# An attention and MLP kernel on one core: a weight load asked for earlier on POOL, and one row's value load moved ahead of a store on SP

## The chip, the core and the metric

The kernel runs on one core of a Trainium2 chip. Its engines are TensorE (PE in the profile; PEld is its weight load), VectorE (DVE), ScalarE (ACT), GpSimd (POOL) and SyncE (SP). Each works through its own instructions in order and waits for the others on semaphores. Transfers are asked for by SP and by POOL, here also once by ScalarE; 16 DMA engines of the core move the bytes. SP's requests and POOL's requests stand in queues of their own (q1 and q0 in the profile). The metric is the time of one execution on the device in microseconds (us); the kernel before takes 300.04 us, the median of 3 runs.

## The reference, cut to what matters

Eight batch rows of 576 tokens go through attention with 8 heads of 64, four of them with a sliding window of 32 and four with a dilated one (every fourth token of 128). The result, 4608 tokens of 512, goes through two matrices with a squared ReLU between them.

```python
mask_plain = (rel >= 0) & (rel < window)
mask_dil = (rel >= 0) & (rel < window * dilation) & (rel % dilation == 0)
masks = np.stack([mask_plain if h < H // 2 else mask_dil for h in range(H)], axis=0)
scores = np.where(masks[None, :, :, :], scores, -1000000000.0)
...
attn = attn / (np.sum(attn, axis=-1, keepdims=True) + 1e-09)
return np.matmul(attn, v).astype(np.float32)
...
h = x @ w_in
r = np.maximum(h, 0.0)
g = r * r
return (g @ w_out).astype(np.float32)
```

q, k and v are float32 of 8 x 8 x 576 x 64, w_in is 512 x 2048 and w_out 2048 x 512, both float32.

## The kernel before

The attention of a batch row is made in parts, and between them stand the matmuls of the MLP, which take chunks of 512 tokens (c = 0 to 8). A chunk first multiplies with w_in (`mm1_tile`, L291), ScalarE takes the ReLU (L300), VectorE squares it (L314, L325), and then it is multiplied with w_out (L332; from chunk 2 on by seven products instead of eight, L443). The order of all work is written out by hand: `run` takes a plan of steps and names ("24:z0" is the first dilated score of a row at step 24), and `pump` puts the matmuls of the MLP between them. No scheduler changes it, so each engine and each queue works in the order of the program text.

A row's q and k come as float16 by POOL's loads, which also convert. For row 0 and row 1 TensorE transposes them (`t_sliding_one`, L573; `t_dilated_one`, L597) into QKTp (sliding) and QKTd (dilated). From row 2 on, `load_whole_sliding_qk` and `keep_dilated_qk` load them, ScalarE and VectorE put the sliding ones in token order (`in_token_order`, tile o, L259 and L261), SP stores that in device memory (`keep_sliding_qk`, dp, L267) and SP's transposing loads bring it back (L279 for QKTd, L275 for QKTp). `turn` issues these steps.

v comes in float32 into two staging tiles, sv for the sliding heads (6 loads for blocks of 96 tokens, `load_sliding_v`, L168) and sd for the dilated ones (`load_dilated_v`: t = 0 at L176, t = 1 at L180, for row 0 also L179). POOL casts them to float16: sv to vp (`cast_own_v` L218, and L222 for the rows that a block shares with the one ahead of it), sd to vd (`cast_dilated_v`, L235, and L237 for the shared rows). There is one sv and one sd, so the loads of the next row wait until POOL has cast the last. The products with v are L693 (sliding, called a0 to a2) and L720 (dilated, d0 and d1 for t = 0, e0 and e1 for t = 1); VectorE divides by the sums (L676, L677), TensorE transposes to x (L742, L757), and ScalarE copies that into xr (L749, L760), which L291 multiplies.

w_in comes in three pieces (`load_w_in`, L192: columns 0 to 511, 512 to 1023, 1024 to 2047) and w_out in four (`load_w_out`, L197), all asked for by POOL and converted to float16. Weights, q, k and POOL's casts so share POOL's program order; v, the stores, the transposing loads and the output share SP's.

`see(x)` (L204) copies one element of x into a tile that nothing reads. It makes POOL wait until x has landed, and so holds back the loads that POOL is asked for behind it. Before this change it is used for row 1's dilated k (L975, ahead of `let_v_go`, which lets SP load row 1's v), and in each chunk for sv and for QKTp ahead of the next row's loads (L1048, L1051).

The order on POOL around the first edit (L896 to L906) is: casts of row 0's first two sliding blocks; two casts of the first half of the dilated v; w_in's first piece; the cast of blocks 2 and 3; w_in's second piece; the shared part; two casts of the second half of the dilated v; w_in's third piece; the casts of blocks 4 and 5. Around the second edit (L990 to L1013), SP's order for row 2 is: dp (two stores), two transposes to QKTd, two to QKTp, sd (two loads), sv (six loads), and then the first output of chunk 0.

Of the kernel before, what the change touches and what calls it, by code (L numbers as in the profile page):

```python
# [17 lines left out]
def kernel(  # L18
# [134 lines left out]
    def load_whole_sliding_qk(b):  # L153
        n = natp.tile([P, HH, 9, D], FP16, name=f"n{b}", tag="n")
        for i, s in ((1, k), (0, q)):
            nc.gpsimd.dma_start(
                out=n[64 * i : 64 * (i + 1)],
                in_=s[b, 0:HH].rearrange("h (p j) d -> p h j d", j=9),
            )
        return n  # L160
# [4 lines left out]
    def load_sliding_v(b, m0=0, m1=NB):  # L165
        for m in range(m0, m1):
            lo = QB * m - PADP
            nc.sync.dma_start(  # L168
                out=sv[PADP:P, m, :, :],
                in_=v[b, 0:HH, lo + PADP : lo + P, :].transpose([1, 0, 2]),  # L170
            )

    def load_dilated_v(b, t):
        vv = v[b, HH:H].rearrange("h (i c) d -> i h (c d)", c=DIL)
        if t == 0:
            nc.sync.dma_start(out=sd[PADD:P, 0, :, :], in_=vv[0:QD])  # L176
            return
        if b == 0:
            nc.sync.dma_start(out=sd[0:PADE, 1, :, :], in_=vv[QD - PADE : QD])  # L179
        nc.sync.dma_start(out=sd[PADE : PADE + QD, 1, :, :], in_=vv[QD:CL])  # L180

    def load_v(b, dilated_first=False):
        if not dilated_first:
            load_sliding_v(b)
        for t in range(2):
            load_dilated_v(b, t)
        if dilated_first:
            load_sliding_v(b)

    def load_w_in(t):  # L190
        f0, f1 = WI[t]
        nc.gpsimd.dma_start(  # L192
            out=wi[t], in_=moe_w_in[:, f0:f1].rearrange("(dh dl) f -> dl dh f", dl=P)
        )
# [7 lines left out]
    def see(landed):  # L202

        nc.gpsimd.tensor_copy(look, landed)  # L204
# [11 lines left out]
    def cast_own_v(b, mp):  # L216
        m = 2 * mp
        nc.gpsimd.tensor_copy(vp[b % 2][:, m : m + 2, :, 0:D], sv[:, m : m + 2, :, :])  # L218

    def cast_shared_v(b, mp):  # L220
        m, m1 = max(2 * mp, 1), 2 * mp + 2
        nc.gpsimd.tensor_copy(vp[b % 2][0:PADP, m:m1, :, 0:D], sv[P - PADP : P, m - 1 : m1 - 1])  # L222

    def cast_sliding_v(b, mp):
        cast_own_v(b, mp)
        cast_shared_v(b, mp)

    def cast_dilated_v(b, t, a):
        c = 2 * a

        def by_class(x):
            return x[:, :, D * c : D * (c + 2)].rearrange("p h (c d) -> p c h d", d=D)

        o = vd[b % 2][:, t, c : c + 2, :, 0:D]
        nc.gpsimd.tensor_copy(o, by_class(sd[:, t]))  # L235
        if t and b > 0:
            nc.gpsimd.tensor_copy(o[0:PADE], by_class(sd[P - PADE : P, 0]))  # L237
# [8 lines left out]
    def keep_dilated_qk(b):  # L246
        d = dpool.tile([2, HH * CL, DIL * D], FP16, name=f"dd{b}", tag="dd")
        for i, src in ((1, k), (0, q)):
            nc.gpsimd.dma_start(
                out=d[i], in_=src[b, HH:H].rearrange("h (i c) d -> (h i) (c d)", c=DIL)  # L250
            )
        return d

    def in_token_order(b, n):
        o = natp.tile([P, 9, HH, D], FP16, name=f"o{b}", tag="o")
        i = n.rearrange("p h j d -> p j h d")
        j = {2: 6, 3: 6, 4: 9}.get(b, 0)
        if j > 0:
            nc.scalar.copy(o[:, 0:j], i[:, 0:j])  # L259
        if j < 9:  # L260
            nc.vector.tensor_copy(o[:, j:9], i[:, j:9])  # L261
        return o

    def keep_sliding_qk(b, o):
        d = dpool.tile([2, S, HH * D], FP16, name=f"dp{b}", tag="dp")
        for i in (1, 0):
            nc.sync.dma_start(  # L267
                out=d[i].rearrange("(p j) x -> p (j x)", j=9),
                in_=o[64 * i : 64 * (i + 1)].rearrange("p j h d -> p (j h d)"),
            )  # L270
        return d

    def transpose_sliding(b, dp):
        for i in (1, 0):
            nc.sync.dma_start_transpose(out=QKTp[b % 2][:, i, :, PADP:], in_=dp[i])  # L275

    def transpose_dilated(b, dd):
        for i in (1, 0):
            nc.sync.dma_start_transpose(out=QKTd[b % 2][:, i, :, KPAD : KPAD + S], in_=dd[i])  # L279
# [321 lines left out]
    def c_dilated_one(b, a, i, p_, eng):  # L601
        copy(
            eng,
            QKTd[b % 2][:, i, a, KPAD : KPAD + S].rearrange("x (c s) -> x c s", s=9),
            p_[:, 0:UW].rearrange("x (s c) -> x c s", c=64),
        )
# [207 lines left out]
    ns0 = [n0[:, 2 * hp : 2 * hp + 2, :] for hp in range(2)]  # L814
# [78 lines left out]
    for a in range(2):  # L893
        t_dilated_one(0, nd0, a, 0, tq[:, a, :])
        c_dilated_one(0, a, 0, tq[:, a, :], nc.scalar)
    cast_sliding_v(0, 0)  # L896
    for a in range(2):
        cast_dilated_v(0, 0, a)
    load_w_in(0)
    cast_own_v(0, 1)  # L900
    load_w_in(1)
    cast_shared_v(0, 1)
# [81 lines left out]
    n, dd = load_whole_sliding_qk(2), keep_dilated_qk(2)  # L984
# [3 lines left out]
            cast_dilated_v(1, t, a)  # L988

    def turn(b, n, dd):  # L990
        dp = keep_sliding_qk(b, in_token_order(b, n))
        if b < 4:
            transpose_dilated(b, dd)
        transpose_sliding(b, dp)
# [13 lines left out]
            parts,  # L1008
        ),
        more=[(25, lambda: turn(2, n, dd))],  # L1010
    )
    load_v(2, True)
    kept[0]()  # L1013


# [23 lines left out]
    for c in range(1, NTOKC):  # L1039
        b = c + 1  # L1040
# [9 lines left out]
        if b + 1 < B:  # L1050
            see(QKTp[b % 2][0:1, 1, 0, PADP : PADP + 1])  # L1051
            if b > CROSS:

                see(xT[(b - 1) % RING][0:1, 1, S - 1 : S])
            n, dd = load_whole_sliding_qk(b + 1), keep_dilated_qk(b + 1)

            def turn_and_load(b=b + 1, n=n, dd=dd):
                turn(b, n, dd)
                load_dilated_v(b, 0)
                load_dilated_v(b, 1)  # L1060
                if b > 3 and b <= CROSS:
                    load_sliding_v(b)

            if b + 1 > 3:
                transpose_dilated(b + 1, dd)
            if b == 3:
                load_sliding_v(3)
            more.append((ORDER[c], turn_and_load))
            if b >= CROSS:
                more.append((38, lambda b=b + 1: load_sliding_v(b)))  # L1070
# [38 lines left out]
```

## Time and profile before

| what | us |
|---|---|
| the runs | 300.04, 299.71, 300.9 |
| the profiled execution | 301.48 |
| its span in the profile | 299.7 |
| first matmul with w_in starts | 20.17 |
| last matmul ends | 296.54 |

The span runs from the first to the last instruction that the profile shows. The busy time of TensorE counts a matmul from its start to an end that is modelled. Mean shares tell little here, as the kernel has a beginning that waits for the first loads, a long dense middle and an end. By page 2, the clock granted to TensorE is full throughout, and the DMA engines are busy for most of the first 200 us:

```profile
PEclk9999999999999999999999999999999999999999
DMA  7999999799999888998999799989124130003013
GB/s 129 205 159 214 210 212 159 154 174 263 196 195 241 179 154 148 215 270 176 186 229 251 144 169 186 255 187 166 72 92 24 39 131 11 0 2 141 3 35 105
```

Each of the 40 slices is 7.5 us. The page's groups of the loads that the change moves, with their number, size and median time from issue to landing:

```profile
sv<-in_v_dram SPq DMA_DIRECT2D x48, 96.0 KB, 4.9
sd<-in_v_dram SPq DMA_DIRECT2D x16, 288.0 KB
...
wi<-in_moe_w_in_dram POOLq DMA_DIRECT2D x2, 512.0 KB, 6.6
wi<-in_moe_w_in_dram POOLq DMA_DIRECT2D x1, 1024.0 KB, 10.2
...
ns<-in_k_dram POOLq DMA_DIRECT2D x2, 144.0 KB, 6.7
```

In a line of a timeline or of the chain, the first number is the start in us from the span's start and the second the length; a bracket at its end gives the idle time of that engine just before, and what ended it.

### The profile page before, as it was taken

The numbers are of one execution on the slowest core, as the hardware profiler recorded it, in microseconds if no ns is written. First come the engines' busy times: TensorE is split into PE (matmuls) and PEld (weight loads), VectorE is DVE, ScalarE is ACT, GpSimd is POOL, SyncE is SP. The second block draws the span as 40 slices with busy tenths as digits, with TensorE's granted clock in tenths as the row PEclk, the third lists the DMA queues.
The fourth block names the chain that finished last, engine by engine and source line by source line (L and its number), as shares of the span: only waits on it lengthen the run. The fifth ranks groups of instructions, "written<-read, shape, count | busy, mean of one in ns | idle before, by whom it ended". The sixth has DMA issues, their size and how long they took to land.

```text
span 299.7 us, 7125 instructions
## 1 busy us (share of the span) xinstructions
PE 287.7 (96%) x2880; PEld 202.7 (68%) x2880; DVE 202.3 (67%) x371; ACT 176.2 (59%) x331; POOL 96.6 (32%) x153
## 2 busy tenths in 40 slices
PE   2899999999999998999999999999999999999995
PEld 2678945565554577656889988558765875785584
DVE  7686646778633997499688867896878624733662
ACT  1668854778548773766646657664766267425611
POOL 8492009403914604752563019308400000000000
PEclk9999999999999999999999999999999999999999
DMA  7999999799999888998999799989124130003013
GB/s 129 205 159 214 210 212 159 154 174 263 196 195 241 179 154 148 215 270 176 186 229 251 144 169 186 255 187 166 72 92 24 39 131 11 0 2 141 3 35 105
DMA packets 73969, 45.59 MB, mean 152 GB/s; under 512 B 56720, under 2 KB 67600, under 8 KB 73744
## 3 DMA queue, kind: packets, MB, share of 16 engines
q1 hardware_dynamic: 66544, 31.37, 49.0%
q0 software_dynamic: 7248, 13.63, 25.7%
q8 instruction: 22, 0.36, 0.5%
q10 hardware_dynamic: 144, 0.13, 0.1%
q14 instruction: 11, 0.09, 0.1%
HBM read 36.83 MB, written 16.52 MB: 178 GB/s over the span
## 4 chain that ended last, share of the span: by engine, by line
PE 72%; DMA 11%; POOL 6%; DVE 5%; issue 2%; SPq 1%; ACT 1%; POOLq 0%; DVEq 0%; ACTq 0%
PE PS L291 34%; PE PS L443 25%; PE PS L332 6%; DMA nd<-in_k_dram 5%; DMA sv<-in_v_dram 3%; DMA sd<-in_v_dram 3%; PE PS L720 2%; PE PS L693 2%; PE PS L653 1%; POOL vp L222 1%; DVE AT L623 1%; POOL vp L218 1%; ACT AT L619 1%; DVE S L429 1%; PE PS L638 1%
## 5 line engine op out<-in xcount | busy, mean ns | idle before, releaser
L291 PE MATMUL PS<-xr,wi 128*128 128x512 f16 (+3 forms) x704 | 133.5, 341 | 0.3 <-ACT xr L749 0.2
L300 ACT ACTIVATE rt<-PS 128x512 f16<-128x512 f32 (+2 forms) x160 | 88.4, 557 | 42.9 <-PE PS L291 40.0
L291 PEld LDWEIGHTS <-wi 128*128 128x128 f16 x704 | 75.8, 113 | 38.5 <-issue 0.5
L325 DVE TENSOR_TENSOR g<-rt 128x1024 f16<-128x1024 f16 (+1 forms) x64 | 45.7, 714 | 28.6 <-ACT rt L300 28.3
L619 ACT ACTIVATE AT<-PS 128x576 f16<-128x576 f32 x64 | 38.4, 652 | 15.5 <-PE PS L653 8.0
L443 PEld LDWEIGHTS <-S 128*128 128x128 f16 x448 | 42.8, 98 | 6.0 <-issue 0.6
L443 PE MATMUL PS<-T,S 128*128 128x256 f16 x336 | 39.6, 273 | 0.0
L443 PEld LDWEIGHTS <-g 128*128 128x128 f16 x336 | 32.2, 98 | 5.6 <-DVE g L325 0.4
L235 POOL CAST vd<-sd 128x512 f16<-128x512 f32 x32 | 23.6, 762 | 36.8 <-DMA sd<-in_v_dram 36.0
L332 PE MATMUL PS<-wo,g 128*128 128x512 f16 x128 | 33.1, 379 | 0.0
L443 PE MATMUL PS<-wo,g 128*128 128x256 f16 x224 | 26.6, 273 | 0.1
L218 POOL CAST vp<-sv 128x512 f16<-128x512 f32 x24 | 17.2, 716 | 23.3 <-DMA sv<-in_v_dram 16.3
L677 DVE TENSOR_TENSOR y<-PS,rcp 72x512 f16<-72x512 f32 (+1 forms) x32 | 22.0, 687 | 1.1
L623 DVE TENSOR_TENSOR AT<-AT,maskd 128x1152 f16<-128x1152 f16 x14 | 11.5, 818 | 15.2 <-ACT AT L619 15.1
L623 DVE TENSOR_TENSOR AT<-AT,maskp 128x1152 f16<-128x1152 f16 x14 | 14.5, 1036 | 10.3 <-ACT AT L619 10.3
L677 DVE TENSOR_TENSOR x<-PS,rcp 96x512 f16<-96x512 f32 (+1 forms) x25 | 16.6, 665 | 0.9
L222 POOL CAST vp<-sv 32x512 f16<-32x512 f32 (+1 forms) x24 | 16.7, 697 | 1.5
L720 PEld LDWEIGHTS <-AT 128*128 128x128 f16 x256 | 11.9, 100 | 6.8 <-DVE y L677 2.0
L332 PEld LDWEIGHTS <-g 128*128 128x128 f16 x128 | 10.3, 98 | 8.0
L429 DVE TENSOR_TENSOR S<-g,S 128x1024 f16<-128x1024 f16 x14 | 10.7, 804 | 7.4 <-PE PS L443 7.4
L676 DVE RECIPROCAL rcp<-PS 96x8 f32<-96x8 f32 (+3 forms) x57 | 11.2, 197 | 4.9 <-PE PS L720 2.9
L443 PE MATMUL PS<-T,g 128*128 128x256 f16 x112 | 14.2, 273 | 0.0
(93 smaller groups left out, 283.2 us busy)
## 6 DMA issues: line engine op xcount, KB each, us to landing
out_dram<-c SPq DMA_DIRECT2D x12, 512.0 KB
sv<-in_v_dram SPq DMA_DIRECT2D x48, 96.0 KB, 4.9
sd<-in_v_dram SPq DMA_DIRECT2D x16, 288.0 KB
dp<-o SPq DMA_DIRECT2D x12, 288.0 KB
wo<-in_moe_w_out_dram POOLq DMA_DIRECT2D x4, 512.0 KB, 14.3
n<-in_k_dram POOLq DMA_DIRECT2D x6, 288.0 KB, 6.0
n<-in_q_dram POOLq DMA_DIRECT2D x6, 288.0 KB, 6.8
dd<-in_k_dram POOLq DMA_DIRECT2D x6, 288.0 KB, 8.1
```

The lines of the kernel that those rows point to most:

```text
L218: nc.gpsimd.tensor_copy(vp[b % 2][:, m : m + 2, :, 0:D], sv[:, m : m + 2, :, :])
L222: nc.gpsimd.tensor_copy(vp[b % 2][0:PADP, m:m1, :, 0:D], sv[P - PADP : P, m - 1 : m1 - 1])
L235: nc.gpsimd.tensor_copy(o, by_class(sd[:, t]))
L291: nc.tensor.matmul(ph[:, o : o + b - a], w_in_of(dmk, ffc), xr[:, dmk, a:b], start=(dmk == 0 and o == 0), stop=(dmk == NDM - 1 and o + b - ...
L300: nc.scalar.activation(rt, ph[:, 0:w], ACTF.Relu)
L325: nc.vector.tensor_mul(g[:, f2 : f2 + 2, o:TOKC], rt[:, :, o:TOKC], rt[:, :, o:TOKC])
L332: nc.tensor.matmul(po, g[:, ffc, o + t * P : o + (t + 1) * P], w_out_of(ffc), start=(ffc == 0), stop=(ffc == NFF - 1),)
L443: nc.tensor.matmul(po[t], lhs(j)[:, t * P : (t + 1) * P], rhs(j), start=j == 0 and not on_top, stop=j == HF - 1, skip_group_check=on_top,)
L619: nc.scalar.activation(AT[:, u + i, 0:UW], ps[:, :, 0 : UW // 2], ACTF.Exp, scale=scale)
L623: nc.vector.tensor_mul(AT[:, u : u + n, 0:UW], AT[:, u : u + n, 0:UW], mask,)
L677: nc.vector.tensor_tensor(out=x, in0=pv[:, :, :, 0:D], in1=rcp[0:w, 0:i, 0:j].unsqueeze(3).to_broadcast([w, i, j, D]), op=ALU.mult,)
L720: nc.tensor.matmul(pav[:, e, h * (D + 2) : h * (D + 2) + D + 1], AT[:, 4 + 2 * a + t, off : off + P], vd[b % 2][:, t, 2 * a + e, h, 0 : D ...
```

## The change

There are two edits. The first puts `load_w_in(0)`, w_in's first piece, ahead of the two casts of the first half of row 0's dilated v on POOL, and ahead of it a `see` of the last sliding k of row 0 (ns0[1], partition 64, where k lies). POOL's order is then: casts of the first two sliding blocks, `see`, w_in's first piece, the two dilated casts, and the rest as before.

The second splits row 2's load of v. The two loads of its dilated half are asked for in `turn`, behind the reordering copies of q and k and ahead of their store; what `load_v(2, True)` asked for behind the transposes is now the sliding half alone. SP's order is then: sd (two loads), dp (two stores), QKTd and QKTp (four transposes), sv (six loads). Other rows keep theirs.

```diff
     cast_sliding_v(0, 0)
+
+    see(ns0[1][64:65, 0, 0:1])
+    load_w_in(0)
     for a in range(2):
         cast_dilated_v(0, 0, a)
-    load_w_in(0)
     cast_own_v(0, 1)
     load_w_in(1)
...
     def turn(b, n, dd):
-        dp = keep_sliding_qk(b, in_token_order(b, n))
+        o = in_token_order(b, n)
+        if b == 2:
+            for t in range(2):
+                load_dilated_v(b, t)
+        dp = keep_sliding_qk(b, o)
         if b < 4:
             transpose_dilated(b, dd)
         transpose_sliding(b, dp)
...
-    load_v(2, True)
+    load_sliding_v(2)
     kept[0]()
```

## The prediction

> **What bounds the kernel now.** I read the page's busy times first, then TensorE's load by stretches, then TensorE's waits, and from each wait the chain back to what releases it.
>
> ```profile
> PE 287.7 (96%) x2880; PEld 202.7 (68%) x2880; DVE 202.3 (67%) x371; ACT 176.2 (59%) x331; POOL 96.6 (32%) x153
> ```
>
> TensorE is busy for 287.7 of 299.7 us, so 12.0 us of idle is all that earlier data could ever give. The same view cut into stretches says where it lies: 6.2 us before the first matmul with w_in (20.17), 0.61 from 20 to 60, nothing from 60 to 108, 1.47 from 108 to 136, 0.45 from 210 to 215, and 3.2 after the last matmul (296.54). The first and last parts wait for the first q and k, for the short chain of row 0, and for the last store; neither edit shortens them. The other idle, 2.53 us, is the ceiling for a gain. Three waits matter, by the timeline (start, length, engine, work, and in brackets the idle before it and what ended it):
>
> ```profile
> 20.17 1.14 PE L291 MATMUL PS<-xr,wi 128*128 128x288 f16 x8 [0.21 <-ACT xr L749]
> 51.88 0.41 PE L693 MATMUL PS<-vp,AT 128*128 128x65 f16 x8 [0.19 <-POOL vp L222]
> 113.29 0.29 PE L693 MATMUL PS<-vp,AT 128*128 128x65 f16 x4 [0.51 <-POOL vp L222]
> ```
>
> The first matmul with w_in is released by ScalarE's copy of x, not by w_in. The other two are released by POOL's casts of v, so what moves v's landing moves them. For row 1 the chain of waits runs back through two long pieces (start, length, what):
>
> ```profile
> 22.14 15.44 DMA nd<-in_k_dram
> ...
> 38.34 6.55 DMA sv<-in_v_dram
> ```
>
> The load of row 1's dilated k stands behind all the weights; when it has landed, `see` (L975) lets POOL free v's loads. Its 15.44 us are queueing: from 16 to 46 us the DMA share is about 1.0 to 1.26 at some 200 GB/s. Ahead of that there is a hole, by the view of 1 us stretches (busy of each engine, then clock, DMA share, GB/s):
>
> ```profile
> 13.00:14.00 1.00, 1.00 (x40) 0.94 (x39) 0.66 (x2) 0.74 (x2) 1.00 (x3) 1.00 0.84 228
> 14.00:15.00 1.00, 1.00 (x14) 0.54 (x14) 1.00 (x3) 0.64 (x1) 1.00 (x2) 1.00 0.63 126
> 15.00:16.00 1.00, 1.00 (x17) 0.71 (x16) 0.96 (x3) 0.60 (x1) 1.00 (x2) 1.00 0.72 24
> 16.00:17.00 1.00, 1.00 (x15) 0.54 (x14) 0.97 (x3) 0.27 (x2) 0.89 (x3) 1.00 0.91 146
> ```
>
> v's loads run dry at about 14.2 and w_in's first bytes come at about 16.1, 2.3 us after their issue at 13.79.
>
> **Part one: w_in's first piece.** POOL before, timeline:
>
> ```profile
> 7.65 0.40 POOL L222 CAST vp<-sv 32x256 f16<-32x256 f32 x1
> 12.44 1.39 POOL L235 CAST vd<-sd 128x512 f16<-128x512 f32 x2 [4.40 <-DMA sd<-in_v_dram]
> 13.79 0.79 POOL L192 DMA_DIRECT2D wi<-in_moe_w_in_dram  x1
> 14.56 0.73 POOL L218 CAST vp<-sv 128x512 f16<-128x512 f32 x1
> ```
>
> Added is one `see`, a copy of one element: 0.18 by the like row at 37.63, 0.24 with the gap behind it. It waits for the last sliding k, issued at 4.54, whose time to landing is 7.3 us (the answer for tile ns: 7.3 and 7.6 for the two issues of that pair; the page's median for k, 6.7, lies between 6.1 and 7.3), so 11.84, 0.48 before sd's 12.32. The piece is then issued at 11.94 + 0.24 = 12.18 instead of 13.79, 1.6 earlier. POOL's 4.40 of idle covers the wait. Behind the waiting `see` stand all of POOL's later casts and loads: the two casts of vd begin at 12.18 + 0.79 = 13.0 instead of 12.44, the first ends at about 13.65, the second at 14.4. Their readers are the products d0 at 13.90 and d1 at 15.29 on TensorE: margins 0.25 and 0.9, so no cost; without that cover each 0.1 that the k lands late costs 0.1. From L218 on POOL is 0.15 earlier (14.4 for 14.56), as it worked in what was idle.
>
> The piece's bytes start at about 12.18 + 2.3 = 14.5, where v's loads end, and fill the hole: all that queues behind moves by up to 1.6. The second piece, issued at 15.1, is ready by 17.4, before the first is through (14.5 + 3.3 = 17.8, from 16.1 to 19.4 before), so the stream doesn't break. Weights gain nothing directly: the pieces landed at 19.39, 22.85 and 28.04, ahead of their first use at about 19.8, 23.5 and 29.5. Row 1's dilated k lands at about 36.0, v's casts end 1.6 earlier, and the wait of 0.19 at 51.88 is gone. Bounds: 0 and -0.19 there; I take -0.19. What the trace does not show is how w_in's bytes and v's last loads share the engines; its lower bound is no cost (the loads are through by then), its upper bound is in the third rival, +2.0. I take 0, as w_in's own row shows 2.3 us from issue to bytes.
>
> **Part two: row 2's dilated v.** Two loads of 288 KB leave SP's queue at 66.14 (0.50 + 0.40, 0.95 with gaps) and go ahead of the store of row 2's q and k.
>
> ```profile
> 56.57 1.19 SPq L267 DMA_DIRECT2D dp<-o  x2
> 57.87 3.92 SPq L279 DMA_TRANSPOSE QKTd<-dd  x2
> 61.89 4.15 SPq L275 DMA_TRANSPOSE QKTp<-dp  x2
> 66.14 0.50 SPq L176 DMA_DIRECT2D sd<-in_v_dram  x1
> 66.69 0.40 SPq L180 DMA_DIRECT2D sd<-in_v_dram  x1
> 67.14 4.05 SPq L168 DMA_DIRECT2D sv<-in_v_dram  x6
> ```
>
> The moved loads wait for POOL's last cast of row 1 (ends 55.66 now, about 54.1 with part one). SP stood waiting for the reordered copy o for 10.6 us before 56.57, so their issue is hidden; were POOL not earlier, the store would slip by 0.05. Their 0.59 MB take 2.8 us at 210 GB/s, from about 56, of which the stretches from 55 to 58 moved 27, 0 and 74 GB/s. The store's bytes may come 1.1 later. Its reader, the transposes at 61.89, wait for TensorE, not for it; their bytes are through by 65 (4 GB/s from 65 to 66), and TensorE first reads QKTp at 72.32, so 6 us cover it.
>
> Sliding v of row 2 starts 1.0 earlier and without 0.59 MB ahead. POOL then doesn't stand 14.70 for sd; its two casts (1.90) go to about 59. The `see` on sv, at 73.38, moves by 1.0 at least and 2.8 at most; I take 2.1. So row 3's load (74.34) comes at about 72.2 and its q at 78 instead of 80.07 (74.97 + 5.1). ScalarE waits for it:
>
> ```profile
> 80.19 1.47 ACT L259 COPY o<-n 128x1536 f16<-128x1536 f16 x1 [2.79 <-DMA n<-in_q_dram]
> 80.20 0.55 DVE L261 COPY o<-n 128x768 f16<-128x768 f16 x1
> 81.68 1.93 SPq L267 DMA_DIRECT2D dp<-o  x2
> ```
>
> ScalarE's half ends at 81.66 and holds the store; VectorE's half is in its busy order and stays at 80.75. So the store gains at most 0.85. From there one link follows the other: transposes, `see` on QKTp (90.89), row 4's loads, whose dilated k is issued at 92.74 and lands 11.8 later, SP's transpose that stood 8.5 us for it (104.59), row 3's sliding v (107.39), its casts (111.83), TensorE at 113.29. The engines are full from 92 to 102, but the same bytes start 0.85 sooner, so I let the link hold. It covers TensorE's idle of 0.12 and 0.51 there. Bounds: 0 if the landing doesn't move, -1.47 if all the idle up to 136 goes; I take -0.63, since the later idle is released by VectorE.
>
> **Sum:** -0.19 + 0 - 0.63 = -0.8. Against the profiled execution's own 301.48 us (span 299.7, 1.78 around it) 300.7. That execution lies 1.44 above the median of 300.04, for which it makes 299.2.
>
> **Rivals.** First, the links break and only the 0.19 is left: 299.85. For it: row 4's loads share the engines with output stores that wait for ScalarE, not for loads. Against it: the engines stood idle at 81 to 83 and at 103 to 106.
>
> Second, more comes: with row 3's v in time the ring of TensorE, ScalarE and VectorE from 113 to 136 loosens and what VectorE releases later goes too: -0.19 - 1.47 - 0.45 = -2.1, so 297.9. For it: these waits stand on one chain behind 113.29. Against it: VectorE is itself busy for 3.97 of 4.00 us from 128 to 132.
>
> Third, slower: w_in takes the engines from v's last loads. Place: the cast of v's blocks 2 and 3 (L218 at 14.56), which landed at 13.3 and 13.6 (5.02 + 8.3, 5.42 + 8.2). Should w_in's bytes start right behind the issue, at 12.97, and go first for all of their 3.3 us, block 3 lands at 16.9; its cast ends at 17.6, the second piece's issue at 18.4, the shared cast (L222, end 16.65 before) at 19.0. TensorE reads that for block 2 at about 17.0, the ninth of its twelve products from 16.68: +2.0 on the way to x and to 20.17, and then on all that follows; 302.0 without the gains, 301.2 with both. It decides from a landing of block 3 later than 14.9 (14.9 + 0.73 + 0.79 + 0.6 = 17.0). Against it: w_in's 2.3 us from issue to bytes.
> The Trainium skill (DMA: Bandwidth & Descriptors, section Queues, rings and completion order) says that each DMA engine takes turns packet by packet between the queue rows that have work. By that rule nothing would go first: block 3's last 0.63 us would take 1.26, its landing be 14.2 and this rival cost nothing, which lowers its chance; whether the bytes of the two meet at all, the trace of before cannot show.
>
> That the change doesn't do what it says has a place too: should sd land ahead of that k, the piece's issue merely delays the casts; this is inside the third rival.
>
> **How the numbers follow.** Forecast 0.44 (own range 298.7 to 299.7), links break 0.15, more 0.22, slower 0.19. The range 297.9 to 301.2 reaches from the second rival to the third with both gains kept. I call 0.5%, 1.5 us, what a measurement can tell from no change; the three runs of before alone spread over 1.2. Faster, below 298.54: most of the second rival (0.19) and the forecast's edge (0.08), 0.27. Slower, above 301.54: the third rival with the gains lost, 0.14. Between: 0.59.
>
> **What would show it.** The piece issued near 12.2 and no hole in the DMA at 15; no wait on TensorE before 20 and its first matmul with w_in at 20.2 (right) or up to 22 (third rival); row 1's dilated k at 36; no wait at 51.9; sd's loads ahead of the store at 54 to 56, QKTp unwaited; row 3's load at 72, the store at 80.8, row 4's dilated k near 103.7 and no wait for vp near 113. A gap on TensorE near 14 (vd late) or at 68 to 72 (QKT late) would make it wrong, and so would a landing of row 4's dilated k that stays at 104.5.

## The result, and the profile after

The changed kernel takes 299.21 us, the median of 22 runs (298.36 to 300.38). The kernel before, run 22 times beside it, takes 300.16 us (299.23 to 301.33). The ratio is 0.9965, with a 95% interval from 0.9951 to 0.9978: a gain of 0.35%, or about 1.05 us. (A ratio here is an estimate from the single runs, not the quotient of the two medians, which is 0.9968.) It is smaller than 0.5%, so by the bound set in the prediction it counts as no change that a few runs could tell, and 299.2 was forecast. The profiled execution of the changed kernel took 299.97 us, with a span of 298.2 (before 301.48 and 299.7). One run in this document, 303.69 us among the 12 of the last kernel of the experiments, was in a slower state, and the ratio there is made without it.

The page's busy times:

```profile
PE 287.3 (96%) x2880; PEld 203.0 (68%) x2880; DVE 202.5 (68%) x371; ACT 176.4 (59%) x331; POOL 98.0 (33%) x154
```

The engines do the same work; POOL has one instruction more, the `see`. Of the 1.5 us between the two spans, 1.1 is idle time of TensorE (12.0 before, 10.9 after); the other 0.4 is in the modelled length of the same 2880 matmuls.

The timeline of POOL after the change (start, length, engine, line, work, and in brackets the idle before it and what ended it):

```profile
11.70 0.22 POOL L204 COPY look<-ns 1x1 f16<-1x1 f16 x1 [3.67 <-DMA ns<-in_k_dram]
11.86 0.79 POOL L192 DMA_DIRECT2D wi<-in_moe_w_in_dram  x1
12.69 1.47 POOL L235 CAST vd<-sd 128x512 f16<-128x512 f32 x2
14.11 0.83 POOL L218 CAST vp<-sv 128x512 f16<-128x512 f32 x1
...
35.58 0.18 POOL L204 COPY look<-nd 1x1 f16<-1x1 f16 x1 [8.40 <-DMA nd<-in_k_dram]
...
69.67 0.18 POOL L204 CAST look<-sv 1x1 f16<-1x1 f32 x1 [10.44 <-DMA sv<-in_v_dram]
70.52 0.64 POOL L156 DMA_DIRECT2D n<-in_k_dram  x1
...
108.22 0.81 POOL L218 CAST vp<-sv 128x512 f16<-128x512 f32 x1 [9.06 <-DMA sv<-in_v_dram]
```

Both edits do what they say. w_in's first piece is issued at 11.86 (13.79 before; 12.18 was forecast). Row 1's dilated k has landed at 35.6 (37.6 before). Row 3's load of k comes at 70.52 (74.34), and the cast of row 3's sliding v at 108.22 (111.83).

The stretches of 1 us after the change (TensorE, its weight load, VectorE, ScalarE, POOL, then the clock, the DMA share and GB/s) show that the hole in the transfers at 14 to 16 is gone:

```profile
14.00:15.00 1.00, 1.00 (x14) 0.50 (x13) 0.97 (x3) 0.17 (x1) 1.00 (x3) 1.00 1.25 231
15.00:16.00 1.00, 1.00 (x15) 0.50 (x12) 0.83 (x3) 0.48 (x1) 0.95 (x2) 1.00 1.25 208
```

Before, these two stretches moved 126 and 24 GB/s.

SP's queue after the change:

```profile
54.04 0.30 SPq L176 DMA_DIRECT2D sd<-in_v_dram  x1
54.44 0.42 SPq L180 DMA_DIRECT2D sd<-in_v_dram  x1
56.22 1.18 SPq L267 DMA_DIRECT2D dp<-o  x2
57.51 3.96 SPq L279 DMA_TRANSPOSE QKTd<-dd  x2
61.56 2.97 SPq L275 DMA_TRANSPOSE QKTp<-dp  x2
64.58 3.47 SPq L168 DMA_DIRECT2D sv<-in_v_dram  x6
...
80.40 1.12 SPq L267 DMA_DIRECT2D dp<-o  x2
...
101.39 2.78 SPq L279 DMA_TRANSPOSE QKTd<-dd  x2
104.27 4.38 SPq L168 DMA_DIRECT2D sv<-in_v_dram  x6
```

The two loads of sd go out while SP would stand waiting for o; the store behind them leaves at 56.22, a little earlier than before (56.57). Row 3's store moves from 81.68 to 80.40, and the transposes that wait for row 4's dilated k from 104.59 to 101.39. What now limits that store is seen in the two halves of o, on ScalarE and on VectorE:

```profile
76.97 1.47 ACT L259 COPY o<-n 128x1536 f16<-128x1536 f16 x1
79.80 0.54 DVE L261 COPY o<-n 128x768 f16<-128x768 f16 x1
```

ScalarE's copy has no wait in brackets any more (2.79 for q before) and ends at 78.44; VectorE's ends at 80.34, and the store leaves 0.06 later.

TensorE's waits in its timeline after the change:

```profile
13.35 0.60 PE L720 MATMUL PS<-vd,AT 128*128 128x65 f16 x8 [0.26 <-POOL vd L235]
19.59 1.14 PE L291 MATMUL PS<-xr,wi 128*128 128x288 f16 x8 [0.30 <-ACT xr L749]
51.30 0.43 PE L693 MATMUL PS<-vp,AT 128*128 128x65 f16 x8 [0.31 <-DVE x L677]
113.97 0.31 PE L653 MATMUL PS<-QKTd 64*128 64x72 f16 x8 [0.44 <-DVE x L677]
```

The two waits for POOL's vp (0.19 at 51.88, 0.51 at 113.29) are gone, and near both places there is one for VectorE's x. A new wait of 0.26 for vd stands at 13.35. From 108 to 136 TensorE is idle for 1.06 us instead of 1.48.

A pair of profiles can't carry a difference of 1 us here. The first transposes of row 0's sliding k on TensorE (L573) start at 8.46 in this execution and at 9.39 in the one of before, though neither edit stands ahead of that k. Which part of the time came from which edit is a question for runs of each edit alone.

### The profile page after: what moved, and what is told of

Its sections match the earlier page's. It is cut to its first block, busy times and chain, and to the rows that moved or that the text cites. A ratio compares the mean times of both kernels' runs of the same rounds, so it can differ in the third digit from the quotient of the medians.

```text
span 298.2 us, 7125 instructions
## 1 busy us (share of the span) xinstructions
PE 287.3 (96%) x2880; PEld 203.0 (68%) x2880; DVE 202.5 (68%) x371; ACT 176.4 (59%) x331; POOL 98.0 (33%) x154
## 4 chain that ended last, share of the span: by engine, by line
PE 81%; DMA 7%; DVE 4%; issue 2%; POOL 2%; SPq 1%; ACT 1%; POOLq 0%
PE PS L291 38%; PE PS L443 24%; PE PS L332 9%; DMA sv<-in_v_dram 5%; PE PS L720 3%; DMA ns<-in_k_dram 2%; PE PS L693 2%; PE PS L638 2%; PE PS L653 1%; POOL vp L218 1%; PE PS L742 1%; DVE AT L623 1%; POOL vp L222 1%; ACT AT L619 1%; SPq L168 1%
## 5 line engine op out<-in xcount | busy, mean ns | idle before, releaser
L332 PEld LDWEIGHTS <-g 128*128 128x128 f16 x128 | 10.3, 97 | 8.0
```

The source lines that it names most:

```text
L332: nc.tensor.matmul(po, g[:, ffc, o + t * P : o + (t + 1) * P], w_out_of(ffc), start=(ffc == 0), stop=(ffc == NFF - 1),)
```

## The experiments

Each result below is a median of 12 runs beside 17 to 35 of the kernel before on the same chip, with the ratio to it and the ratio's 95% interval; the ratio differs from the quotient of the two medians by up to 0.18%. A wait comes from one profiled execution.

**Each edit alone.** The first kernel has only the first edit, the second only the second.

```diff
 e1: turn and load_v(2, True) as before; see and load_w_in(0) ahead of the casts
 e2: casts and load_w_in(0) as before; row 2's dilated v in turn
```

> The first edit alone. Theory (each edit shortens one chain, 0.19 and 0.63 us): 0.2 us faster than before, ratio 0.9985 to 1.000; POOL's casts of row 1's v end 1.5 to 2 us earlier, TensorE's wait of 0.19 for vp near 52 is gone, the waits for vp near 112 to 113 (0.12 and 0.51) are still there, and row 4's dilated k lands where it did (104.5). Rival (the profile of the changed kernel has its first matmul with w_in at 19.59 instead of 20.17, and that comes of the first edit): 0.6 us or more faster, ratio 0.998 or less, first matmul again at 19.6. Rival (the v loads are pushed back): slower, the shared cast of v later than 17.

> The second edit alone. Theory: 0.6 to 0.9 us faster, ratio 0.997 to 0.998; the wait of 0.19 near 52 stays, the wait for vp near 113 is gone or under 0.1, row 3's load at 71 to 72 instead of 74.3, row 4's dilated k lands 1 to 3 us earlier; sd's loads leave SP at 55.7, as POOL's casts of row 1 end where they did. Rival (the gain comes of the first edit): ratio 0.9995 to 1.0005. Rival (the second edit needs the first, since without it sd's loads hold row 2's store): the store slips past 56.6 and less than 0.3 us is gained.

The first edit alone: 300.5 against 300.65, ratio 1.0007 [0.9982, 1.0032]. The second alone: 299.93 against 300.65, ratio 0.997 [0.9947, 0.9993]. TensorE's timeline with the first edit alone:

```profile
13.43 0.59 PE L720 MATMUL PS<-vd,AT 128*128 128x65 f16 x8 [0.53 <-POOL vd L235]
...
111.72 0.29 PE L693 MATMUL PS<-vp,AT 128*128 128x65 f16 x4 [0.26 <-POOL vp L222]
```

The wait at 51 for vp is gone, one of 0.26 near 112 stays, and TensorE loses 0.53 for vd, since POOL now issues w_in ahead of that cast. With the second edit alone:

```profile
50.97 0.41 PE L693 MATMUL PS<-vp,AT 128*128 128x65 f16 x8 [0.27 <-POOL vp L222]
...
111.56 0.29 PE L693 MATMUL PS<-vp,AT 128*128 128x65 f16 x4 [0.26 <-POOL vp L222]
```

Row 3's load is at 71.43 and its store at 80.04, as the theory has it, but 0.26 of the wait for vp at 112 is still there, where under 0.1 had been expected. So the second edit carries the gain that can be measured. The product of the two ratios, 0.9977, lies at the upper edge of the interval of the change (0.9951 to 0.9978).

**Does the second edit's gain pass through row 3's load?** If it does, holding that load back with everything else as changed must undo it. POOL repeats five casts that it has just made, ahead of the loads of row 3's q and k.

```diff
-            for cast in casts[:2]:
+            first = casts[:2]
+            for cast in first:
                 cast()
...
+            if c == 1:
+                for i in range(5):
+                    first[i % 2]()
             n, dd = load_whole_sliding_qk(b + 1), keep_dilated_qk(b + 1)
```

> The changed kernel with row 3's load of q and k held back: POOL repeats five casts that it has just made (the same values to the same places, about 3.3 us) between its looks and that load, which so leaves at 73.8 instead of 70.5, near its time before the change (74.3). Theory (the second edit gains through row 3's load, store, row 4's load and then row 3's sliding v): most of the gain goes, ratio to before 0.998 to 1.000, row 3's store at 81.2 or later, and TensorE's waits for vp near 112 are back. Rival (the gain comes of the traffic that the edit takes out of the stretch from 66 to 70, whatever row 3's load does): ratio 0.9955 to 0.9975.

It took 301.3 against 300.26, ratio 1.0036 [1.0008, 1.0064]: all of the gain is gone and 0.36% more, where 0.998 to 1.000 had been expected. Row 3's load is at 74.46, its store at 82.56, a little later than in the kernel before (74.34 and 81.68). The timeline of ScalarE and TensorE:

```profile
81.06 1.47 ACT L259 COPY o<-n 128x1536 f16<-128x1536 f16 x1 [4.89 <-DMA n<-in_q_dram]
...
78.08 0.41 PE L720 MATMUL PS<-vd,AT 128*128 128x65 f16 x8 [0.29 <-POOL vd L237]
...
112.50 0.29 PE L693 MATMUL PS<-vp,AT 128*128 128x65 f16 x4 [0.51 <-POOL vp L222]
```

TensorE's waits by what it waited for, from 108 to 136 (in all, times, longest), in this kernel:

```profile
PE PS L693 <- POOL vp L222: 0.5, 1, 0.5
PE PS L757 <- DVE y L677: 0.4, 1, 0.4
PE PS L742 <- DVE x L677: 0.3, 1, 0.3
PE PS L720 <- DVE y L677: 0.2, 1, 0.2
```

and in the changed kernel:

```profile
PE PS L653 <- DVE x L677: 0.4, 1, 0.4
PE PS L757 <- DVE y L677: 0.4, 1, 0.4
PE PS L720 <- DVE y L677: 0.2, 1, 0.2
```

The held kernel's list is, row for row, what the same view of the kernel before gives, with sd still ahead of the store and w_in's piece still early. The edit is not clean: the repeated casts also hold back POOL's later casts of row 2's v, and TensorE waits 0.29 for vd at 78.08, which no other profile shows. That is 0.1%, where the ratio moved by 0.7% (0.9965 to 1.0036). So the gain does hang on row 3's load, as far as TensorE's waits account for the casts, and the rival (less traffic from 66 to 70, ratio 0.9955 to 0.9975) is out. That it goes on from there through row 3's sliding v is supported by the list and not isolated: a second profile of the kernel before, shown below, has no wait for vp near 112 at all.

**Is it row 3's sliding v that waits there?** In the kernel before, that load is asked for behind SP's transposes of row 4, which wait for row 4's dilated k. Here the two change places and nothing else does.

```diff
-            if b + 1 > 3:
-                transpose_dilated(b + 1, dd)
             if b == 3:
                 load_sliding_v(3)
+            if b + 1 > 3:
+                transpose_dilated(b + 1, dd)
```

> The kernel before with one other change: SP asks for row 3's sliding v ahead of the transposes that wait for row 4's dilated k (L279 at 104.59), so at about 96 instead of 107.4. It removes the wait for vp near 113 by itself. Theory (that wait and what hangs on it are worth 0.6 us): ratio 0.997 to 0.9985, waits of 0.12 and 0.51 gone. Rival (the wait is only passed on to VectorE's work behind it): ratio 0.9995 to 1.0005. Rival (v's 0.59 MB in front of row 4's dilated k make its transposes late): slower, a wait for QKTd near 115.

It took 300.04 against 300.26, ratio 0.9975 [0.995, 1.0]. The load is asked for at 94.16, the cast of v runs at 104.71 (111.83 before), and the wait near 112 is gone, although row 3's load (73.16) and store (80.91) stay where the second profile of the kernel before has them (73.27 and 80.97). The size, 0.25%, is near what the second edit brings; but the interval reaches 1 and the two medians differ by 0.07% alone, so a gain is not shown.

**Is there more behind it?** If more came from an earlier v or k, further moves of the same kind would add to the gain. One kernel asks for row 3's dilated v early too:

```diff
         o = in_token_order(b, n)
-        if b == 2:
+        if b in (2, 3):
             for t in range(2):
                 load_dilated_v(b, t)
...
                 turn(b, n, dd)
-                load_dilated_v(b, 0)
-                load_dilated_v(b, 1)
+                if b > 3:
+                    load_dilated_v(b, 0)
+                    load_dilated_v(b, 1)
```

> The changed kernel with row 3's dilated v, too, ahead of its store, into the hole in the DMA engines at 78 to 81. Theory (after the change TensorE no longer waits for row 3's v, and VectorE releases what is left of its idle at 112 to 136): no gain over the changed kernel, within 0.2 us, though row 4's dilated k lands 1 to 3 us earlier. Rival (what is left of the idle still hangs on that landing): 0.4 to 1 us faster than the changed kernel.

Row 4's transposes are at 98.67 and row 3's sliding v is cast at 104.94, another 3.3 us earlier, and the ratio is 0.9962 [0.994, 0.9983], like the change itself. A second kernel joins the order of the run before (row 3's sliding v first) to the change, without its `see`:

> The changed kernel without the look ahead of w_in, and with row 3's sliding v asked for ahead of the transposes that wait for row 4's dilated k. Theory (the second edit and this order of SP remove the same wait near 113, so they don't add): ratio 0.995 to 0.9975, as the changed kernel. Rival (they add up): 0.994 or below, the waits of TensorE from 108 to 136 under 0.5 us in sum.

It took 298.99 against 300.5, ratio 0.9959 [0.994, 0.9977]. The two remedies don't add by anything that these runs can tell. With row 3's sliding v cast at 103.25, the waits left from 108 to 136 are all VectorE's (g, x and y), and TensorE is idle there for 1.06 us, as in the changed kernel's profile above. That speaks against the prediction's second rival. The idle itself scatters too much to say more: it is 0.61 in a second profile of the changed kernel and 0.59 with row 3's dilated v early.

**Does w_in's piece take the engines from v?** The prediction's slower rival. Without the `see` the piece is asked for as early as POOL can, in the midst of v's loads.

```diff
-    see(ns0[1][64:65, 0, 0:1])
     load_w_in(0)
```

> The changed kernel without the one-element copy that waits for the last sliding k: w_in's first piece is asked for at about 8.1 instead of 11.9. Theory of the third rival (w_in's bytes take turns with the q, k and v that are still on their way): sd, which landed at 12.3, and the last sliding q land up to 3.3 us later (w_in's own time on the engines), TensorE's first matmul with w_in moves by 0.5 to 3 us, and the kernel is 0.5 to 3 us slower than the changed one. Rival (the engines have room, the copy only costs): as fast as the changed kernel or 0.2 us faster, as the casts of sd then start with its landing.

It took 299.13 against 300.65, ratio 0.9964 [0.9944, 0.9984]: no loss against the changed kernel, where the third rival expected 0.5 to 3 us. POOL's timeline:

```profile
12.48 1.17 POOL L235 CAST vd<-sd 128x512 f16<-128x512 f32 x2 [3.69 <-DMA sd<-in_v_dram]
...
17.05 1.17 POOL L235 CAST vd<-sd 128x512 f16<-128x512 f32 x2 [1.27 <-DMA sd<-in_v_dram]
...
19.43 0.62 POOL L218 CAST vp<-sv 128x512 f16<-128x512 f32 x1 [0.52 <-DMA sv<-in_v_dram]
```

The piece was issued at 8.00, and the bytes do meet: in the profiles of before and of the change the last two of these casts (16.72 and 18.58, 16.36 and 18.21) wait for nothing. But it shows as delays of 1.27 and 0.52 on POOL, and on TensorE as 0.22 for vd at 13.14 and 0.25 for vp at 20.77, not as 3.3 us of v standing behind w_in. The Trainium skill (DMA: Bandwidth & Descriptors, section Queues, rings and completion order) says that an engine takes turns between the queue rows packet by packet; the trace agrees: from 15.0 to 16.5 POOL's queue moved 162 packets (0.17 MB) and SP's 161 (0.05 MB). So v's loads are stretched, and not held back for the whole of a piece; and so is the piece, which landed 10.97 us after its issue, at 18.97, against 17.89 in the changed kernel. What the `see` was to guard against costs nothing that 12 runs can tell.

**What is scatter?** The kernel before was run as if it were a new one, and the changed kernel too.

> The kernel before once more, for its own scatter and a second profile. Theory (the 0.6 us by which the first matmul with w_in starts earlier in the changed kernel's profile is scatter of the first loads' landing, which no edit touches): ratio 0.998 to 1.002, and the first matmul with w_in at 19.2 to 20.2; q and k of row 0 land within 1 us of the first profile's times. Rival (it is the edit's): first matmul at 20.1 to 20.2 again.

> The changed kernel once more, to stand beside the next two on one chip. Theory: ratio to before 0.995 to 0.998, as before; in its profile TensorE waits 0.2 to 0.5 us for vd near 13.3 if row 0's sliding k lands early (transposes of it at 8.3 to 8.6), and not if it lands late (9.3).

The kernel before against itself: 301.0 against 300.26, 1.0016 [0.999, 1.0042]. The changed kernel again: 299.44 against 300.5, 0.9968 [0.9947, 0.9989]. The profiles teach more than the times. TensorE in the second profile of before:

```profile
16.22 0.29 PE L693 MATMUL PS<-vp,AT 128*128 128x65 f16 x4 [0.28 <-POOL vp L222]
...
22.51 1.66 PE L291 MATMUL PS<-xr,wi 128*128 128x288 f16 x12 [0.41 <-DMA wi<-in_moe_w_in_dram]
...
51.07 0.41 PE L693 MATMUL PS<-vp,AT 128*128 128x65 f16 x8 [0.27 <-POOL vp L222]
```

Here the first sliding k is transposed at 8.32 instead of 9.39 and the first matmul with w_in starts at 18.71 instead of 20.17, even earlier than the 19.2 that had been expected. The same kernel now waits for w_in's second piece and, at 16.22, for the shared cast of v, and not at all for vp near 112 (the nearest wait is 0.18 for VectorE's x). From 108 to 136 TensorE is idle for 0.88 us here and 1.48 in the first profile, and for 1.06 and 0.61 in the two profiles of the changed kernel: that stretch scatters by as much as it gains. What is steadier is the time from the first matmul with w_in to the end of the span: 279.5 and 279.4 us in the two profiles of the kernel before, 278.6 and 278.3 in those of the changed kernel, 279.1 with the first edit alone, 278.9 with the second alone and 280.2 with row 3's load held. The second profile of the changed kernel had its k at 8.59 as well, but also an earlier `see` (11.17 for 11.70), so that no wait for vd appeared, against what I had expected of it.

**Is the first edit worth anything?** One kernel keeps w_in where it was and moves the dilated v of rows 2 and 3; one puts the piece between the two casts, for the same two rows; one drops the `see`, for the same two rows.

```diff
 e10: casts, then load_w_in(0), as before; if b in (2, 3)
 e8:  cast_dilated_v(0, 0, 0); load_w_in(0); cast_dilated_v(0, 0, 1); if b in (2, 3)
 e12: load_w_in(0) without see, then the casts; if b in (2, 3)
```

> Dilated v ahead of its store for rows 2 and 3, and w_in's first piece where it was before the change. Theory (the second edit is the whole gain, the first gives back at vd what it gains at vp; row 3's move adds nothing): ratio 0.996 to 0.998, within 0.15% of the changed kernel on the same chip. Rival (the first edit is worth its 0.2 us or more): 0.998 or above. Rival (the first edit costs its wait for vd): 0.9955 or below.

> Both edits, row 3's dilated v ahead of its store too, and w_in's first piece asked for between the two casts of sd, with no look ahead of it. Theory (w_in ahead of both casts makes TensorE wait 0.2 to 0.5 us for vd near 13.3): the first cast starts when sd lands, that wait is gone, and the kernel is 0.1 to 0.4 us faster than the changed one, ratio to before 0.995 to 0.9965. Rival (the wait is taken up by the copies of x that release the first matmul with w_in anyway): as the changed kernel, 0.9965.

> The changed kernel without the look ahead of w_in and with row 3's dilated v ahead of its store, too: the two variants whose profiles were shortest, together. Theory (once row 3's v is in time, VectorE sets the order from 112 to 136, and the start of the kernel differs by the landing of its first loads alone): ratio to before 0.995 to 0.9975, no better than either. Rival (each takes its own 0.2 us): 0.994 or below.

They took 299.57 against 300.5, 299.98 against 300.26 and 299.23 against 300.92; the ratios are 0.9962 [0.9944, 0.998], 0.9973 [0.9948, 0.9997] and 0.9943 [0.9921, 0.9965]. All three intervals overlap, and none lies apart from that of the change. The second ratio is above the range that had been expected, the third below it. The first kernel stands on one chip with the changed kernel's second run: 299.57 and 299.44. TensorE with w_in late:

```profile
23.51 0.68 PE L291 MATMUL PS<-xr,wi 128*128 128x288 f16 x4 [1.23 <-DMA wi<-in_moe_w_in_dram]
```

Of the five profiles with the piece at its old place, two waited on TensorE for w_in (0.41 and 1.23); of the nine with it earlier, none did, but three of these waited for vd (0.22 to 0.53). The median doesn't show whether that nets a gain. The last kernel has the lowest ratio of all; it isn't shown to beat the changed kernel, whose interval reaches from 0.9951.

## Why the prediction held, and where its steps did not

The forecast of -0.8 us came out at about -1.05 (0.35% of 300.16), so the sum is right within its error. That 299.2 was met almost exactly is luck: the kernel before came out at 300.16 and not at the 300.04 that the forecast was taken from. The terms are less right than their sum.

**The second edit, 0 - 0.63: right in its chain, with links sized too small.** Every sign that the prediction listed for it came, some earlier than forecast: sd at 54 to 55, the store unhurt, row 3's load at 70.52 (72.2 was forecast), no wait of ScalarE for q, VectorE's half as the limit of the store, row 4's dilated k at 101.4 (103.7 was forecast), no wait for vp near 113. Holding row 3's load undoes the gain. The term alone measured -0.3% [-0.53, -0.07], some 0.9 us; 0.63 lies inside, so the term isn't shown to be too small, but its links are. The mis-sized one is "So the store gains at most 0.85" and what was built on it: the store moved by 1.28, in the first pair of profiles and in the second (80.97 to 79.69), as VectorE's half didn't stay at 80.75 but ended at 80.34. The v behind it came 3.6 us earlier in the first pair (111.83 to 108.22) and 2.35 in the second (109.78 to 107.43), and not 0.85. Part of the 3.6 is scatter: row 4's dilated k took 11.8 us to land in the first profile of before and 10.4 in the second, with 10.3 and 10.0 in the changed kernel. The wait for vp near 113 was 0.51 in one profile of before and absent in the other. How much of the 0.9 lies outside this one wait isn't settled.

**The first edit, -0.19: its wait went, its gain did not show.** The measured 1.0007 allows from -0.54 to +0.96 us. All five profiles with the old order wait for vp near 51 (0.19 to 0.43), and of the nine with the piece earlier one does (0.19, without the `see`). Two statements failed. "Margins 0.25 and 0.9, so no cost" was read from an execution whose first k came 0.9 us late, when TensorE reached d0 at 13.90. With the k at its more common time TensorE is ready by 12.9 to 13.1, and the wait was 0.26 in the changed kernel and 0.53 with the first edit alone. "Weights gain nothing directly" came from the same execution: with TensorE earlier, w_in's second piece is on the edge, and two profiles with the old order waited 0.41 and 1.23 for it. These two errors have opposite signs. And the 0.19 at 51.88 was no net gain in the end: TensorE stood 0.31 at the same place for VectorE's x, in both profiles of the changed kernel and in three of its variants (0.31 to 0.34). Two readings of the trace were wrong, with no effect on the sum. Row 1's dilated k doesn't stand behind all the weights: two of w_out's four pieces are asked for behind it (23.18 and 28.34). And the 2.3 us "from issue to bytes" are the time until the rate rises: POOL's queue moves its first packets of w_in about 1.5 us after the issue, 18 of them from 15 to 16.

**The rivals.** As ratios to 300.04 they are 0.9994 (the links break, 299.85), 0.9929 (more comes, 297.9) and 1.004 or more (slower), and all three lie outside the measured 0.9951 to 0.9978. That the links break is further refuted by the held load. More did not come with further moves either: with row 3's sliding v cast 6.9 and 8.6 us earlier than before (104.94 and 103.25 against 111.83), no more was gained that can be measured. The last kernel of the experiments (0.9943, from 0.9921) alone leaves room for it. That w_in takes the engines from v's last loads is refuted by the run without the `see`, in which it was given the best chance: the piece went out 4 us earlier than in the change, its packets took turns with v's instead of going first, and TensorE lost 0.2 to 0.25 twice.

**The signs at the start** were half right. The piece came near 12.2 and the hole at 15 closed, as said; the first matmul with w_in came at 19.59 and not at 20.2, and there was a wait before 20. The prediction had named a gap on TensorE near 14 for vd as a sign that it is wrong, and this gap came, 0.26 at 13.35; it was too small to turn the sum. As the kernel before has its first matmul with w_in at 18.71 in its second profile, that start tells when k lands and is no effect of the change.

## What to carry to other kernels

When a queue works in order, look for a load that stands behind an instruction which waits for something else: here moving 0.59 MB ahead of a store that SP was idle for anyway, with no byte less to move, was worth 0.3% (0.07 to 0.53). Follow such a gain through every link to the wait that ends, hold one link back to test it, and expect the next engine to set the rest. A margin below 1 us in the first 20 us of this kernel can't be read from one profile: look at a second execution before an edit is costed at nothing there.

## What the runs showed of the hardware

- The landing of the very first loads varies between executions by about 1 us with nothing changed ahead of it: TensorE's first transposes of the sliding k start between 8.32 and 9.39 over 14 profiles, two of which (9.39 and 9.34) are late; the other twelve lie between 8.32 and 8.85. The late start of the first matmul with w_in follows it (20.17 and 20.38 against 18.69 to 19.59 in the others), and which wait shows up in the first 25 us changes with it.
- w_in's 512 KB asked for in the midst of v's loads slowed those by 1.27 and 0.52 us at the places where POOL waited, and not by the whole length of the piece. While both had work, from 15.0 to 16.5, the two queues moved the same number of packets (162 and 161), and so POOL's, with the larger packets, three times the bytes (0.17 and 0.05 MB).
- A load asked for earlier into busy engines need not land earlier: w_in's first piece was issued 3.9 us earlier there than in the changed kernel (8.00 for 11.86) and landed 1.1 us later (18.97 for 17.89).
- Row 4's dilated k, 288 KB in each kernel, needed 7.5 to 8.5 us from issue to landing in the four profiled kernels that ask for row 3's dilated v (0.59 MB) ahead of row 3's store, and 10.0 to 11.8 in the other ten profiles, in which that v is asked for shortly before it: what a transfer takes hangs on what is under way beside it.
